# Another order of the attention units, and routing logits in fp32 by token

## The chip, the cores and the metric

The kernel runs on one core of a Trainium2 chip, alone. The metric is the time of one execution in device microseconds. Engines are named as the profile names them: PE is TensorE (PEld its weight loads), DVE is VectorE, ACT is ScalarE, POOL is GpSimd, SP is SyncE, whose queue issues most DMA transfers.

## The reference

Three stages in a row, all in fp32.

1. Gated linear attention, 4 batches, 8 heads, 768 positions, 48 wide: `state = f[t] * state + k[t] v[t]^T`, `y[t] = q[t] state`, with `f = sigmoid(f_logit)`.
2. A dense feed-forward layer on the 3072 tokens of 384 features (8 heads of 48): `h = x @ w_in` (384 to 2048), `g = h * clip(h + 3, 0, 6) / 6`, `x2 = g @ w_out`.
3. A mixture of 8 experts, one for each token:

```python
logits = x @ w_gate
e_idx = np.argmax(logits, axis=1)
gate_w = softmax(logits)[e_idx]
eom = 1.0 / (1.0 + np.exp(-(x @ w_output_gate)))
out[mask] = gate_w[mask, None] * eom[mask, e, None] * (np.maximum(x[mask] @ w1[e], 0.0) @ w2[e])
```

`x` in this third stage is the second stage's result. A logit that is off by a little can choose another expert, so the logits need full precision.

## The kernel before, in words

**Products in three parts.** Large matmuls run on fp32r operands, an fp32 number being split into a high and a low part (`split`, L122), and a product is three matmuls: high by high, high by low, low by high (`mm3`, L309 to L312).

**Attention units.** Tokens are cut into 8 blocks of 384 (half a batch). For each block there are four units, one for each pair of heads (`attention`, L212 to L306). A unit loads its f, k, q and v (L221, L223), makes decays on ScalarE and VectorE (L227 to L242), transposes k (L248), multiplies k by q (L253), masks (L260), multiplies k by v (L266), updates the state (L274 to L284) and sums the output `py` in PSUM (L291, L294), with head 0 of the pair in rows 0 to 47 and head 1 in rows 64 to 111. The output is split into high and low by ScalarE (L300) and VectorE (L301). The first products of a unit wait for that subtraction of the unit before (`freed`, L256).

**Where the output goes.** The feed-forward layer wants 384 features as 3 parts of 128 rows. Pairs 0, 1 and 2 are written straight into part 0, 1 and 2 of the block's tile `xx`, all 128 rows, of which 48 to 63 and 112 to 127 hold nothing. Pair 3 goes to a tile `yx`, and six DMA transfers on SP (L302 to L306) move 16 rows each from there into those free rows. Then every part is full. The pairs are taken in the order 0, 1, 2, 3.

**Feed-forward blocks.** `mlp` (L314) goes through 16 groups f of 128 hidden features: nine up matmuls over the three parts of `xx` into a PSUM bank `ph` (two banks in turn), `relu6` (ACT L347, DVE L348, ACT L349, DVE L350), and two groups later nine down matmuls into three accumulators (L323 to L325). Between groups the units of the coming blocks are written into the program: `UNITS = (-5, 0, 5, 9)` (L460) puts the second, third and fourth unit of block b + 1 at f = 0, 5 and 9, and the first unit of block b + 2 at f = 11. The units of block 0 and the first of block 1 come ahead of all blocks, in a prefix (L462 to L469), together with the first seven parts of the feed-forward weights; these are loaded as raw words into two buffers (L132) and converted by ScalarE and VectorE (L138 to L146). The other parts follow in the first groups of block 0.

**Routing.** After a block, `route` (L414) calls `choose` (L357). The accumulators are scaled into `row` (L363), transposed part by part (L366), and split into `xh` and `xl` (L367, L368). The logits come with the features on the output's rows: the stationary operand is the gate's weights, 32 columns (16 high beside 16 low), and the moving one is 384 tokens (L374, six matmuls). They are copied (L379), transposed back to tokens in three small steps (L382), copied and added (L385, L387). The weights for it are split beforehand (L470 to L476). Then come the choice of expert, a slot for each token, and three indirect DMA transfers that scatter the rows to DRAM (L436).

**Experts.** After the last block each expert's rows are loaded, transposed (L553) and put through two layers, the fullest expert first, its first 256 rows ahead of the others; those are transposed inside the last route (`meanwhile`). A general branch (L716 on), which these inputs don't enter, uses `choose` as well, with `keep`.

**What sets the order.** Instructions are given to a planner in program order; at compile time it fixes the order on each engine by that priority and by its own estimates of durations (`schedule_with_timeline_sim`, L868). `after_all` adds a wait, `in_turn` fixes an order on TensorE, `issue_after` places loads behind a given instruction. On the chip each engine follows its list. PSUM has three accumulator banks, two for `ph`, and three (`ps_m`) shared by attention, routing and transposes.

Of the kernel before, what the change touches and what calls it, by code (L numbers as in the profile page):

```python
# [10 lines left out]
F32 = mybir.dt.float32  # L11
F32R = mybir.dt.float32r
# [5 lines left out]
ALU = mybir.AluOpType  # L18
# [4 lines left out]
P = 128  # L23
# [3 lines left out]
KD = DM // P  # L27
FF = 2048
NF = FF // P
E = 8  # L30
FE = 1024
NFE = FE // P
TB = 384
# [15 lines left out]
def fused(ctx: ExitStack, tc: tile.TileContext, q, k, fl, v, vt, w_in, w_out, wg, w1, w2, out):  # L49
    nc = tc.nc  # L50
    const = ctx.enter_context(tc.tile_pool(name="const", bufs=1))
# [3 lines left out]
    ps_m = ctx.enter_context(tc.tile_pool(name="ps_m", bufs=3, space=PSUM))  # L55
# [17 lines left out]
    ident = const.tile([P, P], F32, name="ident")  # L73
# [33 lines left out]
    nc.gpsimd.memset(three, 3.0)  # L107
    gcmin = const.tile([R, 4 * NB], F32, name="gcmin")

    wgs = [const.tile([P, KD, 4 * E], F32R, name=f"wgs{i}") for i in range(2)]  # L110

    second = ExitStack()
    rtp = second.enter_context(tc.tile_pool(name="rtp", bufs=2))
# [5 lines left out]
    at1 = attc.enter_context(tc.tile_pool(name="at1", bufs=1, side="right"))  # L119
# [28 lines left out]
    def first_weights(pool):  # L148
        return [pool.tile(sh, F32R, name=n) for n, sh in (("wih", [P, KD, FF]), ("wil", [P, KD, FF]),
                                                          ("woh", [P, NF, DM]), ("wol", [P, NF, DM]))]  # L150
# [48 lines left out]
    sbds = []  # L199
    for i in range(2):  # L200
        t = at1.tile([R, NCH, 2, 64], F32, name=f"sbd{i}")
        nc.gpsimd.memset(t, 0.0)
        sbds.append(t)
    state, ready, freed = {}, [], []
# [7 lines left out]
    def attention(blk, pr, xx):  # L212
        b, half = divmod(blk, 2)
        n = 4 * blk + pr
        sbd = sbds[n % 2]
        qt = at2.tile([R, NCH, CH], F32, tag="qt", name="qt", bufs=3)
        kt = at2.tile([R, NCH, CH], F32, tag="kt", name="kt")
        xt = at2.tile([R, NCH, CH], F32, tag="xt", name="xt", bufs=3)
        vs = at2.tile([P, NCH, 2, 64], F32, tag="vs", name="vs")
        for t, src in ((xt, fl), (kt, k), (qt, q)):  # L220
            nc.sync.dma_start(out=t.rearrange("p c t -> p (c t)"),  # L221
                              in_=src[4 * b + pr, :, half * TB:(half + 1) * TB])
# [74 lines left out]
        in_turn(products)  # L297

        yx = xx[:, :, pr, :] if pr < 3 else at1.tile([P, 2, TB], F32R, tag="yx", name="yx")
        nc.scalar.copy(yx[:, 0, :], py)  # L300
        freed[1:] = [nc.vector.tensor_tensor(out=yx[:, 1, :], in0=py, in1=yx[:, 0, :].bitcast(F32), op=ALU.subtract)]  # L301
        if pr == 3:  # L302
            for j in range(KD):
                for x in range(2):
# [52 lines left out]
    def choose(pool, acc, keep=None, meanwhile=None):  # L357

        row = pool.tile([P, 3, ROW], F32, tag="row", name="row", bufs=1)
        xh, xl = (pool.tile([P, KD, TB], F32R, tag=n, name=n, bufs=1) for n in ("xTh", "xTl"))  # L360
        for t in range(3):
            ts_ = slice(t * P, (t + 1) * P)
            nc.scalar.activation(row[:, t, 0:DM], acc[t], AF.Copy, scale=1.0 / 6.0)  # L363
            px = ps_m.tile([P, KD, P], F32, tag="m", name="px")
            for kt in range(KD):
                nc.tensor.transpose(px[:, kt, :], row[:, t, kt * P:(kt + 1) * P], ident)  # L366
            nc.scalar.copy(xh[:, :, ts_], px)  # L367
            nc.vector.tensor_tensor(out=xl[:, :, ts_], in0=px, in1=xh[:, :, ts_].bitcast(F32), op=ALU.subtract)  # L368
        if keep is not None:
            keep(xh, xl)  # L370
        pl = ps_m.tile([4 * E, TB], F32, tag="m", name="pl")
        for i, (w, x) in enumerate(((wgs[0], xh), (wgs[1], xl))):
            for kt in range(KD):
                nc.tensor.matmul(pl, lhsT=w[:, kt, :], rhs=x[:, kt, :], start=i == 0 and kt == 0,  # L374
                                 stop=i == 1 and kt == KD - 1)
        if meanwhile is not None:
            meanwhile()
        lgT = pool.tile([4 * E, TB], F32, tag="lgT", name="lgT", bufs=1)
        nc.scalar.copy(lgT, pl)  # L379
        pt = ps_m.tile([P, 3, 4 * E], F32, tag="m", name="pt")  # L380
        for t in range(3):
            nc.tensor.transpose(pt[:, t, :], lgT[:, t * P:(t + 1) * P], ident[:4 * E, :4 * E])  # L382
        sm = lambda name, shape, dt=F32: pool.tile([P] + shape, dt, tag=name, name=name)
        lg2 = sm("lg2", [3, 4 * E])
        nc.vector.tensor_copy(lg2, pt)  # L385
        lg = sm("lg", [3, 2 * E])
        nc.vector.tensor_tensor(out=lg, in0=lg2[:, :, 0:2 * E], in1=lg2[:, :, 2 * E:], op=ALU.add)  # L387
        mx = sm("mx", [3, 1])
        nc.vector.tensor_reduce(out=mx, in_=lg[:, :, 0:E], op=ALU.max, axis=AX.X)
        dl = sm("dl", [3, E])  # L390
        nc.vector.tensor_tensor(out=dl, in0=lg[:, :, 0:E], in1=mx.to_broadcast([P, 3, E]), op=ALU.subtract)
        ex = sm("ex", [3, E])
        nc.scalar.activation(ex, dl, AF.Exp)
        se = sm("se", [3, 1])
        nc.vector.tensor_reduce(out=se, in_=ex, op=ALU.add, axis=AX.X)

        cand = sm("cand", [3, E])
        nc.vector.scalar_tensor_tensor(out=cand, in0=dl, scalar=0.0, in1=wts, op0=ALU.is_equal, op1=ALU.mult)
        m2 = sm("m2", [3, 1])
        nc.vector.tensor_reduce(out=m2, in_=cand, op=ALU.max, axis=AX.X)  # L400
        oh = sm("oh", [3, E], BF16)
        nc.vector.tensor_tensor(out=oh, in0=wts, in1=m2.to_broadcast([P, 3, E]), op=ALU.is_equal)

        zz = sm("zz", [3, E])
        nc.vector.tensor_tensor(out=zz, in0=lg[:, :, E:], in1=oh, op=ALU.mult)
        zs = sm("zs", [3, 1])
        nc.vector.tensor_reduce(out=zs, in_=zz, op=ALU.add, axis=AX.X)
        nc.scalar.activation(zs, zs, AF.Exp, scale=-1.0)
        nc.vector.tensor_scalar_add(zs, zs, 1.0)
        nc.vector.scalar_tensor_tensor(out=zs, in0=se, scalar=1e-9, in1=zs, op0=ALU.add, op1=ALU.mult)  # L410
        nc.vector.reciprocal(row[:, :, DM:DM + 1], zs)
        return row, oh
# [37 lines left out]

    xts = {}

    def att_unit(blk, pr):
        if pr == 0:
            xts[blk] = blkp.tile([P, 2, KD, TB], F32R, tag="xx", name="xx")
        attention(blk, pr, xts[blk])

    wfirst = first_weights(m1)

    UNITS = (-5, 0, 5, 9)  # L460
    parts = [part for i in range(NF // 4) for part in load_first(cv, i, *wfirst)]
# [5 lines left out]
    for pr in range(4):  # L467
        if UNITS[pr] < -1:
            att_unit(1, pr)  # L469
    wraw = at1.tile([P, KD, 4 * E], F32, name="wraw")  # L470
    nc.gpsimd.memset(wraw, 0.0)
    nc.sync.dma_start(out=wraw[:, :, 0:2 * E], in_=wg)
    nc.scalar.copy(wgs[1], wraw)
    nc.scalar.copy(wgs[0][:, :, 0:2 * E], wraw[:, :, 0:2 * E])
    nc.gpsimd.tensor_tensor(out=wgs[0][:, :, 2 * E:], in0=wraw[:, :, 0:2 * E],
                            in1=wgs[1].bitcast(F32)[:, :, 0:2 * E], op=ALU.subtract)  # L476

    def fill(e):
        fills.append(nc.sync.dma_start(out=xs_d[e * NT:e * NT + 384].rearrange("(j p) c -> p j c", p=P),
# [236 lines left out]
    with tc.If(general > 0):  # L716
# [41 lines left out]
        with ExitStack() as es:  # L758
            gp = es.enter_context(tc.tile_pool(name="gw", bufs=1))
            wg1 = first_weights(gp)  # L760
            for i in range(NF // 4):
                for part in load_first(gp, i, *wg1):
                    part()
            with tc.For_i(0, NB, 1) as nb:
                xg = gp.tile([P, KD, TB], F32, tag="xg", name="xg")
                xth = gp.tile([P, KD, TB], F32R, tag="xth", name="xgh")
                xtl = gp.tile([P, KD, TB], F32R, tag="xtl", name="xgl")
                yv = ya_d.rearrange("h (b r) p t -> (h b) r p t", r=4)
                for j in range(KD):
                    for x in range(2):  # L770
                        for dst, pr, src in ((64 * x, j, D * x), (64 * x + D, 3, D * x + 16 * j)):
                            n = D if pr < 3 else 16
                            nc.sync.dma_start(out=xg[dst:dst + n, j, :],
                                              in_=yv[bass.ds(nb, 1), pr, src:src + n].rearrange("a p t -> p (a t)"))
                split(xth, xtl, xg, nc.gpsimd)

                def keep(xh, xl):
                    x2 = gp.tile([P, KD, TB], F32, tag="x2", name="x2")
                    nc.vector.tensor_tensor(out=x2, in0=xh.bitcast(F32), in1=xl.bitcast(F32), op=ALU.add)
                    nc.sync.dma_start(out=x2_d[bass.ds(nb, 1)].rearrange("a p k t -> p (a k) t"), in_=x2)  # L780

                row, oh = choose(gp, mlp(gp, xth, xtl, *wg1, NF, relu6), keep)
                gs = gp.tile([P, E, 3, 2], F32, tag="gs", name="gs")
                nc.vector.tensor_copy(gs[:, :, :, 0], row[:, None, :, DM].to_broadcast([P, E, 3]))
                nc.vector.tensor_copy(gs[:, :, :, 1], oh.rearrange("p t e -> p e t"))
                for e in range(E):
                    nc.sync.dma_start(out=gs_d[e, bass.ds(nb, 1)].rearrange("a p t c -> p (a t) c"), in_=gs[:, e])
# [81 lines left out]
```

## Time and profile before

| | |
|---|---|
| median of 3 runs | 866.75 us (864.46 to 869.58) |
| the profiled execution | 864.98 us |
| its span in the profile | 863.3 us |
| mean granted clock of TensorE | 0.963 |
| TensorE busy | 805.9 us |
| VectorE busy | 526.4 us |
| ScalarE busy | 396.4 us |
| instructions | 14521 |

The span runs from the first to the last instruction; 1.7 us of the profiled execution lie around it. A timeline row gives the start in us from the span's start, the duration, the engine, the line, the operation, output and inputs by the program's names, the shape, how many instructions of the kind follow each other (then the duration is that of all), and in brackets the idle time of the engine before it with what ended it. `SPq` rows are DMA issues. Matmuls overlap their successors, so a matmul's own duration is longer than its share of the engine's time, which is read from start to start. [...]

### The profile page before, as it was taken

The numbers are of one execution on the slowest core, as the hardware profiler recorded it, in microseconds if no ns is written. First come the engines' busy times: TensorE is split into PE (matmuls) and PEld (weight loads), VectorE is DVE, ScalarE is ACT, GpSimd is POOL, SyncE is SP. The second block draws the span as 40 slices with busy tenths as digits, with TensorE's granted clock in tenths as the row PEclk, the third lists the DMA queues.
The fourth block names the chain that finished last, engine by engine and source line by source line (L and its number), as shares of the span: only waits on it lengthen the run. The fifth ranks groups of instructions, "written<-read, shape, count | busy, mean of one in ns | idle before, by whom it ended". The sixth has DMA issues, their size and how long they took to land.

```text
span 863.3 us, 14521 instructions
## 1 busy us (share of the span) xinstructions
PE 805.9 (93%) x5503; PEld 746.4 (86%) x5503; DVE 526.4 (61%) x1118; ACT 396.4 (46%) x843; POOL 62.3 (7%) x103
## 2 busy tenths in 40 slices
PE   7558998999998999999899999999999999999995
PEld 3338987998997998999799899899898999999994
DVE  6999975569554578654567843463464452554631
ACT  5556654447434455633445533453354342453520
POOL 2000000200010010010010010010100011101111
PEclk9558999999999999999999999999999999999998
DMA  6565495023021113110211200050254163255600
GB/s 200 169 187 156 153 283 168 29 68 106 1 70 52 31 62 92 48 61 26 65 63 42 57 29 11 14 174 20 68 178 157 34 207 131 92 185 183 216 26 28
DMA packets 42412, 85.01 MB, mean 98 GB/s; under 512 B 5954, under 2 KB 29795, under 8 KB 42333
## 3 DMA queue, kind: packets, MB, share of 16 engines
q1 hardware_dynamic: 39052, 74.50, 28.5%
q0 software_dynamic: 3280, 9.49, 3.0%
q8 instruction: 45, 0.74, 0.4%
q14 instruction: 35, 0.28, 0.1%
HBM read 65.77 MB, written 16.26 MB: 95 GB/s over the span
## 4 chain that ended last, share of the span: by engine, by line
PE 47%; DVE 4%; DMA 3%; ACT 2%; issue 1%; SPq 0%; POOL 0%; POOLq 0%; DVEq 0%; ACTq 0%
PE ph L310 7%; PE ph L312 7%; PE ph L311 7%; PE acc L323 3%; PE acc L324 3%; PE acc L325 3%; PE yacc L311 2%; PE yacc L312 2%; PE yacc L310 2%; DMA raw<-in_w 2%; PE yrow L599 1%; PE yrow L595 1%; PE yrow L598 1%; PE px L553 1%; PE py L291 1%
## 5 line engine op out<-in xcount | busy, mean ns | idle before, releaser
L310 PE MATMUL ph<-xx,wih 128*128 128x384 f32 x384 | 134.0, 349 | 9.8 <-DMA xx<-yx 6.5
L312 PE MATMUL ph<-xx,wil 128*128 128x384 f32 x384 | 132.6, 345 | 0.0
L311 PE MATMUL ph<-xx,wih 128*128 128x384 f32 x384 | 131.9, 344 | 0.0
L347 ACT ACTIVATE gf<-ph,three 128x384 f32<-128x384 f32 x128 | 73.6, 580 | 126.1 <-PE ph L312 122.9
L324 PE MATMUL acc<-wol,gh 128*128 128x384 f32 x384 | 129.8, 338 | 0.0
L323 PE MATMUL acc<-woh,gh 128*128 128x384 f32 x384 | 129.4, 337 | 0.3 <-ACT gh L349 0.3
L325 PE MATMUL acc<-woh,gl 128*128 128x384 f32 x384 | 122.0, 337 | 0.0
L348 DVE SCALAR_TENSOR_TENSOR gf<-gf,ph 128x384 f32<-128x384 f32 x128 | 70.1, 551 | 80.8 <-ACT gf L347 80.0
L350 DVE TENSOR_TENSOR gl<-gf,gh 128x384 fp32r<-128x384 f32 x128 | 70.4, 552 | 34.8 <-ACT gh L349 34.2
L354 DVE SCALAR_TENSOR_TENSOR hl<-ph,hh 128x256 fp32r<-128x256 f32 (+7 forms) x72 | 39.0, 542 | 82.2 <-ACT hh L353 77.2
L349 ACT CAST gh<-gf 128x384 fp32r<-128x384 f32 x128 | 65.3, 512 | 51.2 <-DVE gf L348 49.5
L310 PEld LDWEIGHTS ph<-xx,wih 128*128 128x128 f32 x384 | 74.2, 193 | 13.6 <-DMA xx<-yx 7.3
L353 ACT ACTIVATE hh<-ph 128x256 fp32r<-128x256 f32 (+7 forms) x72 | 34.6, 481 | 109.3 <-PE ph L312 109.3
L312 PEld LDWEIGHTS ph<-xx,wil 128*128 128x128 f32 x384 | 74.0, 193 | 0.9 <-issue 0.5
L311 PEld LDWEIGHTS ph<-xx,wih 128*128 128x128 f32 x384 | 74.0, 193 | 0.3
L323 PEld LDWEIGHTS acc<-woh,gh 128*128 128x128 f32 x384 | 72.1, 188 | 1.1 <-ACT gh L349 0.6
L324 PEld LDWEIGHTS acc<-wol,gh 128*128 128x128 f32 x384 | 72.1, 188 | 1.1 <-issue 0.7
L325 PEld LDWEIGHTS acc<-woh,gl 128*128 128x128 f32 x384 | 71.2, 188 | 0.8 <-issue 0.3
L310 PE MATMUL ph<-xh,w1h 128*128 128x256 f32 (+7 forms) x216 | 71.9, 334 | 0.0
L311 PE MATMUL ph<-xl,w1h 128*128 128x256 f32 (+7 forms) x216 | 71.7, 333 | 0.0
L312 PE MATMUL ph<-xh,w1l 128*128 128x256 f32 (+7 forms) x216 | 71.5, 332 | 0.0
L436 POOL DMA_INDIRECT xs_d<-row,sli x24 | 24.4, 1019 | 558.6 <-DVE sli L431 406.7
(168 smaller groups left out, 1471.0 us busy)
## 6 DMA issues: line engine op xcount, KB each, us to landing
raw<-in_w SPq DMA_DIRECT2D x23, 512.0 KB, 6.1
raw<-in_w SPq DMA_DIRECT2D x30, 384.0 KB, 3.4
vs<-in_v SPq DMA_DIRECT2D x32, 192.0 KB, 2.5
raw<-in_w_in SPq DMA_DIRECT2D x12, 512.0 KB, 4.2
raw<-in_w_out SPq DMA_DIRECT2D x12, 512.0 KB, 3.7
xt<-in_fl SPq DMA_DIRECT2D x32, 168.0 KB, 3.1
kt<-in_k SPq DMA_DIRECT2D x32, 168.0 KB, 2.3
qt<-in_q SPq DMA_DIRECT2D x32, 168.0 KB, 2.6
```

Of the source, the lines that this page charges most:

```text
L310: nc.tensor.matmul(ps, lhsT=wh, rhs=xh, start=first, stop=False)
L311: nc.tensor.matmul(ps, lhsT=wh, rhs=xl, start=False, stop=False)
L312: nc.tensor.matmul(ps, lhsT=wl, rhs=xh, start=False, stop=last)
L323: nc.tensor.matmul(acc[t], lhsT=gh[:, ts_], rhs=w2h[:, f, :], start=f == 0, stop=False)
L324: nc.tensor.matmul(acc[t], lhsT=gh[:, ts_], rhs=w2l[:, f, :], start=False, stop=False)
L325: nc.tensor.matmul(acc[t], lhsT=gl[:, ts_], rhs=w2h[:, f, :], start=False, stop=f == nf - 1)
L347: nc.scalar.activation(gf, ph, AF.Relu, bias=three)
L348: nc.vector.scalar_tensor_tensor(out=gf, in0=gf, scalar=6.0, in1=ph, op0=ALU.min, op1=ALU.mult)
L349: nc.scalar.copy(gh, gf)
L350: nc.vector.tensor_tensor(out=gl, in0=gf, in1=gh.bitcast(F32), op=ALU.subtract)
L353: return (nc.scalar.activation(gh, ph, AF.Relu).ins, nc.vector.scalar_tensor_tensor(out=gl, in0=ph, scalar=0.0, in1=gh.bitcast(F32), op0=A ...
L354: nc.vector.scalar_tensor_tensor(out=gl, in0=ph, scalar=0.0, in1=gh.bitcast(F32), op0=ALU.max, op1=ALU.subtract).ins)
```

## The change

The pairs are taken in the order 0, 1, 3, 2, so that the six transfers follow the third unit. Pair 2, now last, is written head by head into the rows that are its own, since the rows between may have been filled already; pair 0 and 1 are written as before. The two buffers `sbds` alternate by the number of units so far and not by the pair.

In `choose`, x2 is turned once and kept in fp32 (`xT`, one VectorE copy for each third), and the logits are fp32 matmuls with 128 tokens stationary and the 16 columns of the gate's weights moving, so that they come out by token. The split of the gate's weights, the second copy, the three small transposes and the addition go.

```diff
@@ fused @@
-    wgs = [const.tile([P, KD, 4 * E], F32R, name=f"wgs{i}") for i in range(2)]
+    wgs = const.tile([P, KD, 2 * E], F32, name="wgs")
@@ attention @@
-        sbd = sbds[n % 2]
+        sbd = sbds[len(ready) % 2]
...
-        nc.scalar.copy(yx[:, 0, :], py)
-        freed[1:] = [nc.vector.tensor_tensor(out=yx[:, 1, :], in0=py, in1=yx[:, 0, :].bitcast(F32), op=ALU.subtract)]
+        freed[1:] = []
+
+        for rows in heads if pr == 2 else (slice(0, P),):
+            nc.scalar.copy(yx[rows, 0, :], py[rows])
+            freed.append(nc.vector.tensor_tensor(out=yx[rows, 1, :], in0=py[rows], in1=yx[rows, 0, :].bitcast(F32),
+                                                 op=ALU.subtract))
@@ choose @@
-        xh, xl = (pool.tile([P, KD, TB], F32R, tag=n, name=n, bufs=1) for n in ("xTh", "xTl"))
+        xt = pool.tile([P, KD, TB], F32, tag="xT", name="xT", bufs=1)
...
-            nc.scalar.copy(xh[:, :, ts_], px)
-            nc.vector.tensor_tensor(out=xl[:, :, ts_], in0=px, in1=xh[:, :, ts_].bitcast(F32), op=ALU.subtract)
+            nc.vector.tensor_copy(xt[:, :, ts_], px)
+        pl = ps_m.tile([P, 3, 2 * E], F32, tag="m", name="pl")
+        for t in range(3):
+            for kt in range(KD):
+                nc.tensor.matmul(pl[:, t, :], lhsT=xt[:, kt, t * P:(t + 1) * P], rhs=wgs[:, kt, :], start=kt == 0,
+                                 stop=kt == KD - 1)
...
-        pl = ps_m.tile([4 * E, TB], F32, tag="m", name="pl")
-        for i, (w, x) in enumerate(((wgs[0], xh), (wgs[1], xl))):
-            for kt in range(KD):
-                nc.tensor.matmul(pl, lhsT=w[:, kt, :], rhs=x[:, kt, :], start=i == 0 and kt == 0,
-                                 stop=i == 1 and kt == KD - 1)
...
-        lgT = pool.tile([4 * E, TB], F32, tag="lgT", name="lgT", bufs=1)
-        nc.scalar.copy(lgT, pl)
-        pt = ps_m.tile([P, 3, 4 * E], F32, tag="m", name="pt")
-        for t in range(3):
-            nc.tensor.transpose(pt[:, t, :], lgT[:, t * P:(t + 1) * P], ident[:4 * E, :4 * E])
...
-        lg2 = sm("lg2", [3, 4 * E])
-        nc.vector.tensor_copy(lg2, pt)
         lg = sm("lg", [3, 2 * E])
-        nc.vector.tensor_tensor(out=lg, in0=lg2[:, :, 0:2 * E], in1=lg2[:, :, 2 * E:], op=ALU.add)
+        nc.vector.tensor_copy(lg, pl)
@@ att_unit, prefix @@
-    def att_unit(blk, pr):
-        if pr == 0:
+    def att_unit(blk, i):
+        pr = PAIRS[i]
+        if i == 0:
...
+    PAIRS = (0, 1, 3, 2)
...
-    wraw = at1.tile([P, KD, 4 * E], F32, name="wraw")
-    nc.gpsimd.memset(wraw, 0.0)
-    nc.sync.dma_start(out=wraw[:, :, 0:2 * E], in_=wg)
-    nc.scalar.copy(wgs[1], wraw)
-    nc.scalar.copy(wgs[0][:, :, 0:2 * E], wraw[:, :, 0:2 * E])
-    nc.gpsimd.tensor_tensor(out=wgs[0][:, :, 2 * E:], in0=wraw[:, :, 0:2 * E],
-                            in1=wgs[1].bitcast(F32)[:, :, 0:2 * E], op=ALU.subtract)
+    nc.sync.dma_start(out=wgs, in_=wg)
```

## Rows read from the trace of the kernel before

**Rows 1.** The page, its first part: busy time, share of the span and instructions by engine.

```profile
PE 805.9 (93%) x5503; PEld 746.4 (86%) x5503; DVE 526.4 (61%) x1118; ACT 396.4 (46%) x843; POOL 62.3 (7%) x103
```

**Rows 2.** Busy time by stage: stretch, its length, each engine's busy us, clock, DMA share, GB/s.

```profile
20.00:64.40 44.40, 23.61 (x157) 15.94 (x152) 41.81 (x86) 24.55 (x54) 0.00 (x0) 0.56 0.62 183
...
75.00:140.00 65.00, 61.79 (x464) 57.84 (x463) 57.64 (x118) 39.70 (x85) 0.00 (x0) 0.99 0.70 214
...
140.00:150.00 10.00, 9.26 (x44) 8.81 (x45) 3.89 (x9) 3.39 (x7) 0.00 (x0) 0.83 0.27 77
...
414.00:424.00 10.00, 9.21 (x58) 8.37 (x59) 8.21 (x16) 6.16 (x16) 0.00 (x0) 0.83 0.34 93
...
605.00:640.00 35.00, 33.33 (x274) 31.54 (x275) 17.45 (x52) 13.96 (x35) 4.92 (x5) 1.00 0.42 138
```

**Rows 3.** The waits of TensorE: who waited for whom, us in total, times, longest us.

```profile
PE ph L310 <- DMA xx<-yx: 6.5, 5, 2.6
...
PE ph L310 <- DVE gf L348: 2.9, 5, 1.0
...
PE pa L253 <- ACT kn L250: 1.8, 3, 0.8
```

**Rows 4.** The timeline where block 1 starts: start us, us, instruction, count, idle time before.

```profile
140.32 0.41 PE L310 MATMUL ph<-xx,wih 128*128 128x384 f32 x1 [2.58 <-DMA xx<-yx]
...
141.12 0.52 PE L311 MATMUL ph<-xx,wih 128*128 128x384 f32 x1
```

**Rows 5.** The timeline where block 5 starts.

```profile
411.55 0.94 PE L253 MATMUL pa<-qt,kb 48*128 48x128 f32 x12 [0.78 <-ACT kn L250]
...
414.38 0.66 PE L310 MATMUL ph<-xx,wih 128*128 128x384 f32 x1 [1.41 <-DMA xx<-yx]
```

**Rows 6.** The timeline of the prefix and of block 0's start.

```profile
47.14 7.20 SPq L132 DMA_DIRECT2D raw<-in_w_out  x3
...
60.79 0.54 DVE L301 TENSOR_TENSOR yx<-py,yx 128x384 fp32r<-128x384 f32 x1
...
61.36 3.94 SPq L305 DMA_DIRECT2D xx<-yx  x6
...
64.43 0.66 PE L310 MATMUL ph<-xx,wih 128*128 128x384 f32 x1 [0.75 <-DMA xx<-yx]
```

**Rows 7.** Instructions of the tile xx: ns min/median/max, first and last start.

```profile
L300 ACT CAST xx<-py x24: 457/480/483, 17.5 to 536.0; 128x384 fp32r<-128x384 f32 x24
...
L301 DVE TENSOR_TENSOR xx<-py,xx x24: 533/552/558, 18.0 to 536.5; 128x384 fp32r<-128x384 f32 x24
```

**Rows 8.** Groups by line and shape on TensorE: busy us, mean ns, idle before.

```profile
L253 PE MATMUL pa<-qt,kb 48*128 48x128 f32 x384 | 32.2, 303 | 4.0 <-ACT kn L250 1.8 <-ACT th L227 1.4 <-ACT th L230 0.8
```

**Rows 9.** The timeline of TensorE around the logits: block 0's route, then the last one.

```profile
135.62 0.42 PEld L291 LDWEIGHTS py<-at,vs 128*64 128x64 f32 x8 [0.25 <-issue]
...
147.70 0.69 PE L374 MATMUL pl<-xTh,wgs 128*32 128x384 f32 x3
...
148.22 0.34 PE L310 MATMUL ph<-xx,wih 128*128 128x384 f32 x1
...
608.85 0.19 PEld L311 LDWEIGHTS ph<-xl,w1h 128*128 128x128 f32 x1
...
608.96 0.19 PEld L312 LDWEIGHTS ph<-xh,w1l 128*128 128x128 f32 x1
...
609.21 0.19 PEld L312 LDWEIGHTS ph<-xh,w1l 128*128 128x128 f32 x1
...
609.53 0.37 PE L382 MATMUL pt<-ident,lgT 32*128 32x32 f32 x3
```

**Rows 10.** The timeline of the last route and of what follows it.

```profile
606.83 0.71 PE L374 MATMUL pl<-xTh,wgs 128*32 128x384 f32 x3 [0.59 <-ACT xTh L367]
...
608.33 0.47 ACT L379 COPY lgT<-pl 32x384 f32<-32x384 f32 x1 [0.16 <-PE pl L374]
...
628.67 0.39 PE L311 MATMUL yacc<-hl,w2h 128*128 128x256 f32 x1 [0.82 <-DVE hl L354]
```

More of the change, by code (lines that the diff above doesn't have):

```diff
@@ L366, in choose @@
                 nc.tensor.transpose(px[:, kt, :], row[:, t, kt * P:(kt + 1) * P], ident)
-            nc.scalar.copy(xh[:, :, ts_], px)
-            nc.vector.tensor_tensor(out=xl[:, :, ts_], in0=px, in1=xh[:, :, ts_].bitcast(F32), op=ALU.subtract)
-        if keep is not None:
-            keep(xh, xl)
-        pl = ps_m.tile([4 * E, TB], F32, tag="m", name="pl")
-        for i, (w, x) in enumerate(((wgs[0], xh), (wgs[1], xl))):
-            for kt in range(KD):
-                nc.tensor.matmul(pl, lhsT=w[:, kt, :], rhs=x[:, kt, :], start=i == 0 and kt == 0,
-                                 stop=i == 1 and kt == KD - 1)
+            nc.vector.tensor_copy(xt[:, :, ts_], px)
[4 more added lines that the diff above has]
+                                 stop=kt == KD - 1)
+        if keep is not None:
+            keep(xt)
         if meanwhile is not None:
             meanwhile()
-        lgT = pool.tile([4 * E, TB], F32, tag="lgT", name="lgT", bufs=1)
-        nc.scalar.copy(lgT, pl)
-        pt = ps_m.tile([P, 3, 4 * E], F32, tag="m", name="pt")
-        for t in range(3):
-            nc.tensor.transpose(pt[:, t, :], lgT[:, t * P:(t + 1) * P], ident[:4 * E, :4 * E])
         sm = lambda name, shape, dt=F32: pool.tile([P] + shape, dt, tag=name, name=name)
-        lg2 = sm("lg2", [3, 4 * E])
-        nc.vector.tensor_copy(lg2, pt)
         lg = sm("lg", [3, 2 * E])
-        nc.vector.tensor_tensor(out=lg, in0=lg2[:, :, 0:2 * E], in1=lg2[:, :, 2 * E:], op=ALU.add)
+        nc.vector.tensor_copy(lg, pl)
         mx = sm("mx", [3, 1])
@@ L775, in fused, with keep @@
                 split(xth, xtl, xg, nc.gpsimd)
-                def keep(xh, xl):
-                    x2 = gp.tile([P, KD, TB], F32, tag="x2", name="x2")
-                    nc.vector.tensor_tensor(out=x2, in0=xh.bitcast(F32), in1=xl.bitcast(F32), op=ALU.add)
+                def keep(x2):
                     nc.sync.dma_start(out=x2_d[bass.ds(nb, 1)].rearrange("a p k t -> p (a k) t"), in_=x2)
```

## The prediction, made before the changed kernel was run

> **What bounds the kernel now.** I read the page first, then busy time by stage, then the waits, then the timeline at the block starts. TensorE is busy for 93% of the span [rows 1], so the question is where the other 7% lies. [...] From 75 us on TensorE is busy nearly throughout (61.79 of 65.00 us). After that an edit is worth what it takes from or adds to TensorE's own work, or what idle time it closes.
>
> The waits name that idle time [rows 3]: five times the first up matmul of a block (L310) waits for the transfers that move the rows of heads 6 and 7 (yx to xx), 6.5 us in all, at most 2.6. It comes with a second loss. Before block 1 TensorE sits idle for 2.58 us; soon after, the same matmul's record grows to 0.52 us and the clock of that stretch is 0.83 instead of 1.00 [rows 2, 4]. Block 5 has the same 0.83 after idle times of 0.78 and 1.41 us [rows 2, 5]. At 0.83 over 10 us, 1.7 us of full-speed work is lost; twice makes 3.4 us.
>
> **The change part by part.**
>
> *The order of the units.* At the start of block 0 the last copy of the fourth unit starts at 60.79 and lasts 0.54, the six transfers go out from 61.36 to 65.30, and the first up matmul starts at 64.43 after a wait of 0.75 [rows 6]. With pair 3 third in line its six transfers leave about one unit earlier, so they have landed long before the block starts, and the first six up matmuls (parts 0 and 1 of xx) depend on nothing of the last unit. Gain: the 6.5 us, and the 3.4 us of clock if the idle time was what cost it. Late next is the last unit's own copy, which only the third part of xx needs. Ends: nothing gained if that copy takes the transfers' place, all of it otherwise. I take all, since six matmuls lie ahead of the part that needs it: 9.9 us.
>
> *Where the transfers go.* In every block the six issues (3.94 us of SP's queue, rows from 61.36 [rows 6]) pass ahead of whatever loads were behind the third unit. Later blocks have slack there: no weights are loaded in them. In the prefix they land among the raw weight loads, three of which issue from 47.14 over 7.20 us, paced by their two buffers [rows 6]. Behind them ScalarE and VectorE would wait for raw weights. I take zero, as the queue itself is waiting for buffers there; ends 0 and 3.9 us.
>
> *Head by head.* Pair 2's copy becomes two on ScalarE and two on VectorE with the same columns on 48 rows. A copy of all 128 rows takes 0.48 us, the subtraction 0.55 [rows 7]; the added pair has the same 384 columns on fewer rows, so I charge the full price, 0.48 and 0.55 per block. What hides it is the time before the block starts; what doesn't is the next unit's first products (L253), which wait for this very subtraction: before block 5 that wait is already open (0.78) [rows 5], and three such waits come to 1.8 us [rows 3], of which I put two at a block's end. Two times 0.55 = +1.1 us; ends 0 (the planner puts up matmuls there) and three times 1.03.
>
> *Logits, TensorE.* Removed per block: six matmuls with 384 moving columns, three of which take 0.52 us from their first start to the next matmul's start (147.70 to 148.22), so 1.04; and three small transposes, some 0.3 [rows 9]. Together 1.35 us. Added: nine fp32 matmuls with 128 stationary and only 16 moving columns. An fp32 matmul here is two instructions: the program's 192 products at L253 (32 units, three chunks, two heads) stand in the trace as 384 [rows 8], with a weight load each. So 18 loads of 128 columns with almost nothing to hide behind. Loads of that size start 0.11 us apart at the closest (608.85, 608.96) and 0.125 apart on the next two (to 609.21) [rows 9]. 18 times 0.11 is 2.0 us, so +0.63 per block; at 0.125, +0.9. The other end: eight loads of half the columns take 0.42, or 0.053 each [rows 9], which would make it 0.95 us and a gain of 0.4. I take 0.11, the row of the same size. In seven blocks TensorE has no idle time to absorb it: +4.4 us (ends -2.8 and +6.3).
>
> *Logits, the other engines.* Three casts to xh (0.48 each, as in [rows 7]) and the copy of lgT (0.47 [rows 10]) leave ScalarE; on VectorE three subtractions become three copies of the same shape (same price), and two small steps become one. ScalarE thus does 1.9 us less just where a block starts, and where up matmuls wait for the activation to give back a bank: 2.9 us in five waits [rows 3]. I take a quarter of it, -0.7; ends 0 and -2.9.
>
> *The last route.* Here TensorE waits: 0.59 us ahead of the logits, which hides their 0.63 extra, and 0.82 us at 628.67 after the rows that this route scatters came late [rows 10]. The chain from acc to slots loses a cast of 0.48, the copy of 0.47 and the transposes, over 1 us. I take -0.8; ends 0 and -1.4.
>
> *Preparing the gate weights.* One DMA straight into place; two narrow casts leave ScalarE, each at most the 0.48 of a copy four times as wide [rows 7]. I take zero, because VectorE bounds the prefix [rows 2] and hides it; ends 0 and -1.0.
>
> **Sum.** -6.5 - 3.4 + 1.1 + 4.4 - 0.7 - 0.8 = -5.9 us. On the profiled execution's 864.98 that is 859.1. The median of the runs is 866.75, 1.8 above it; the forecast goes with the median: 860.9.
>
> **The rivals.**
>
> *More than that.* The planner now has six ready up matmuls at each boundary and puts them into the waits at L253 (1.8 [rows 3]), the 1.1 isn't paid, and block 0 starts some 2 us sooner because TensorE idles in the prefix. Another -4.9: 856.0. For: those matmuls hang on nothing late. Against: older units come first in the program.
>
> *The last copy takes the transfers' place.* VectorE is in order and busy; before block 0 its copy was late. Half of the 9.9 stays: 865.9.
>
> *Raw loads late in the prefix.* The 3.9 us of issues hold up weights on the engine that bounds that stage: 864.8.
>
> *The clock falls in the route.* Nine transposes and 18 short matmuls give TensorE 3 us in which few columns stream, once per block. The price is 1.7 us per fall, as in blocks 1 and 5 [rows 2]; eight falls cost 13.6: 874.5, slower. It decides from six falls on (10.2 us, the forecast's gain plus 4.3). Against: nine transposes and two idle times in the last route left the clock at 1.00 (605 to 640) [rows 2]. [...]
>
> *Loads that hide behind nothing.* If each of the 18 pays its load's full 0.19 us [rows 9], a block pays 3.4 and not 2.0: +16.3 in place of +4.4 over eight blocks, 872.8. Against: loads of 0.19 that start 0.11 apart [rows 9]. [...]
>
> *The transfers stay last.* The planner may still let unit and transfers end at the block's start: no 9.9, 870.8.
>
> **How the numbers follow.** Forecast 0.38; more 0.20; last copy 0.13; raw loads 0.13; clock 0.08; transfers stay last 0.05; loads 0.03. The range 854 to 869 leaves out the last three and a tail of the second. A measurement of this kernel can tell about 0.5%, 4.3 us, from no change: faster is under 862.4, slower over 871.1. Faster: two thirds of the forecast's case (0.26), all of the second, and small parts of the next two (0.07): 0.53. Slower: most of the clock's case, the loads' and half of the transfers' (0.12), and a little for a plan that came out badly in some other way: 0.14. The rest, 0.33, is the same.
>
> **What would show it.** In the changed profile: no row "PE ph L310 <- DMA xx<-yx"; a clock of 1.00 in the ten us after blocks 1 and 5 start; the six transfers of a block well before its first up matmul; 18 logit instructions per block with loads some 0.11 us apart, about 2 us in all; ScalarE's busy time down by about 12 us. It is wrong if first up matmuls wait for L301 as long as they did for the transfers, if VectorE waits longer for raw weights between 45 and 60 us, or if the granted clock dips after the routes.

## The result, and the profile after

The changed kernel takes 857.81 us (855.66 to 858.24, 4 runs) beside 865.61 for the kernel before (864.46 to 869.58): a ratio of 0.9908, 95% interval 0.9882 to 0.9934. The forecast was 860.9; it started from 866.75, the median of three runs before, of which this comparison has four. The profiled execution took 857.86, its span is 856.1; before it was 864.98, so 7.1 us went. By stage of the two traces:

| stage | before, us | after, us |
|---|---|---|
| start to the first up matmul | 64.4 | 50.6 |
| block 0's up matmuls | 65.0 | 79.6 |
| block 0's last up to the last route | 474.9 | 470.3 |
| of that: TensorE idle / lost to the lower clock / the rest | 14.1 / 3.4 / 457.4 | 6.6 / 3.4 / 460.3 |
| last route to the end | 258.9 | 255.6 |

(Idle is the sum of the gaps ahead of TensorE's instructions; lost is time at half clock, halved.) Block 0 starts 14 us sooner and its up matmuls end 0.8 us later: by these rows the earlier start is worth nothing (a run below tries it). The 7.1 us lie in the blocks (4.6) and behind the last route (3.3), less that 0.8.

The changed kernel's page, busy time by engine, answers to [rows 1]:

```profile
PE 807.9 (94%) x5575; PEld 753.9 (88%) x5575; DVE 528.3 (62%) x1118; ACT 388.0 (45%) x817; POOL 59.3 (7%) x101
```

TensorE has 72 instructions more, nine a block, and is busy 2.0 us longer; ScalarE lost 8.4 us, where about 12 were forecast. The waits of TensorE over the whole span, answering to [rows 3] (in all, times, longest):

```profile
PE py L291 <- ACT sbd L284: 12.4, 6, 4.8
PE ph L314 <- DVE gf L352: 8.9, 4, 5.6
...
PE ph L314 <- DMA xx<-yx: 2.3, 1, 2.3
PE pa L253 <- DVE xx L304: 1.7, 1, 1.7
...
```

The transfers are waited for once, ahead of block 0, instead of five times. Waits for the state that a unit needs (sbd) were there before too; from block 0's last up matmul to the last route the kernel before has

```profile
PE ph L310 <- DMA xx<-yx: 5.8, 4, 2.6
PE py L291 <- ACT sbd L284: 2.7, 3, 1.2
```

and the changed kernel has 5.6 us for sbd, in three waits, each some 8 us behind the start of block 2, 4 or 6, where the next block's first unit needs that state. So 5.8 us of waits went there and 2.9 came. And the clock falls again. Busy time by stretch, answering to [rows 2]; the columns are those of [rows 2]:

```profile
20.00:50.60 30.60, 18.46 (x128) 12.11 (x125) 28.00 (x57) 16.19 (x34) 0.00 (x0) 0.60 0.61 181
...
132.00:142.00 10.00, 10.00 (x89) 8.85 (x87) 3.34 (x8) 3.57 (x8) 0.00 (x0) 1.00 1.04 352
...
211.80:215.20 3.40, 3.40 (x29) 3.07 (x26) 2.21 (x5) 2.13 (x5) 0.00 (x0) 0.50 0.31 82
```

Block 1's start (132.1) now has full clock and no idle time, against 0.83 in [rows 2]. But from 211.8 it is 0.50 for 3.4 us, right behind a 1.85 us wait for sbd (the row at 211.54 below), and again at 484.9 behind one of 1.95. Two falls before, two after: 3.4 us lost in both.

The logits and the last route, answering to [rows 9, 10] (start us, us, instruction, count):

```profile
601.06 1.31 PE L370 MATMUL px<-ident,row 128*128 128x128 f32 x9 [0.28 <-ACT row L367]
601.64 1.49 DVE L371 COPY xT<-px 128x384 f32<-128x384 f32 x3 [3.14 <-PE px L370]
602.25 1.41 PEld L375 LDWEIGHTS pl<-wgs,xT 128*128 128x128 f32 x12
602.25 1.51 PE L375 MATMUL pl<-wgs,xT 128*128 128x16 f32 x12
...
603.87 0.74 PE L375 MATMUL pl<-wgs,xT 128*128 128x16 f32 x6
604.46 0.42 PE L546 MATMUL px<-ident,xr 128*128 128x128 f32 x2
604.81 0.20 DVE L383 COPY lg<-pl 128x48 f32<-128x48 f32 x1
```

Nine products are 18 instructions with 18 loads. From first start to the next matmul's start a run of six takes 0.59 us here (603.87 to 604.46), and one of twelve 1.26 in the route behind block 1 (220.03 to 221.29, below), so 1.85 us a block against some 1.35 before. The route is shorter: from row's first copy (600.5) to lg's end it is 4.5 us, where it took 6.1.

The two timelines below are of the start of block 3, in the changed kernel, and then of the route that follows block 1:

```profile
269.41 0.47 ACT L303 CAST xx<-py 48x384 fp32r<-48x384 f32 x1 [1.96 <-PE py L294]
...
269.84 0.44 ACT L250 COPY kn<-pk 128x336 f32<-128x336 f32 x1
269.91 0.55 DVE L304 TENSOR_TENSOR xx<-py,xx 48x384 fp32r<-48x384 f32 x1 [1.88 <-ACT xx L303]
...
271.39 0.47 ACT L303 CAST xx<-py 48x384 fp32r<-48x384 f32 x1
...
271.98 0.56 DVE L304 TENSOR_TENSOR xx<-py,xx 48x384 fp32r<-48x384 f32 x1
...
275.82 0.94 PE L253 MATMUL pa<-qt,kb 48*128 48x128 f32 x12
```

```profile
211.54 0.49 PE L291 MATMUL py<-at,vs 128*64 128x128 f32 x4 [1.85 <-ACT sbd L284]
...
214.10 1.40 PE L370 MATMUL px<-ident,row 128*128 128x128 f32 x6
...
219.18 0.49 PE L370 MATMUL px<-ident,row 128*128 128x128 f32 x3
...
220.03 1.41 PE L375 MATMUL pl<-wgs,xT 128*128 128x16 f32 x12
...
221.29 0.42 PE L315 MATMUL ph<-xx,wih 128*128 128x384 f32 x1
```

The last unit's second copy (271.39) comes 2 us after its first: kn and an activation (270.78) stand between them on ScalarE. The next unit's first products (L253) need both subtractions. They start at 275.82, which is 3.3 us after the second has ended (272.54), and TensorE is busy until then: what puts them there is the order on TensorE, which was fixed at compile time, and not a wait on the chip. In the second timeline a first unit that is late in this way meets the route: its products (py, 211.54) stand right in front of the route's transposes (214.10), with which they share the three ps_m banks, and the last three transposes come 5 us after the first six.

### The profile page after: what moved, and what is told of

Its sections match the earlier page's. It is cut to its first block, busy times and chain, and to the rows that moved or that the text cites. A ratio compares the mean times of both kernels' runs of the same rounds, so it can differ in the third digit from the quotient of the medians.

```text
span 856.1 us, 14631 instructions
## 1 busy us (share of the span) xinstructions
PE 807.9 (94%) x5575; PEld 753.9 (88%) x5575; DVE 528.3 (62%) x1118; ACT 388.0 (45%) x817; POOL 59.3 (7%) x101
## 4 chain that ended last, share of the span: by engine, by line
PE 80%; DVE 11%; DMA 4%; issue 2%; ACT 2%; SPq 1%; POOL 0%; POOLq 0%; DVEq 0%; ACTq 0%
PE ph L314 11%; PE ph L316 11%; PE ph L315 11%; PE acc L327 7%; PE acc L328 7%; PE acc L329 7%; PE py L291 3%; PE yacc L315 3%; PE yacc L316 3%; PE yacc L314 3%; PE pa L253 2%; PE py L294 2%; PE pl L375 2%; DMA raw<-in_w_in 1%; PE yrow L592 1%
## 5 line engine op out<-in xcount | busy, mean ns | idle before, releaser
L327 PE MATMUL acc<-woh,gh 128*128 128x384 f32 x384 | 131.2, 342 | 0.0
L329 PE MATMUL acc<-woh,gl 128*128 128x384 f32 x384 | 124.3, 337 | 0.2 <-DVE gl L354 0.2
L354 DVE TENSOR_TENSOR gl<-gf,gh 128x384 fp32r<-128x384 f32 x128 | 70.6, 552 | 31.7 <-ACT gh L353 30.9
```

The source lines that it names most:

```text
L327: nc.tensor.matmul(acc[t], lhsT=gh[:, ts_], rhs=w2h[:, f, :], start=f == 0, stop=False)
L329: nc.tensor.matmul(acc[t], lhsT=gl[:, ts_], rhs=w2h[:, f, :], start=False, stop=f == nf - 1)
L354: nc.vector.tensor_tensor(out=gl, in0=gf, in1=gh.bitcast(F32), op=ALU.subtract)
```

## The experiments

All ratios are to the kernel before in runs on the same chip. "Stage" is block 0's last up to the last route, "route" the mean time from row's first copy to lg's end over the six routes of blocks 0 to 5. Every kernel got its own order at compile time, so an edit can move more than what it names.

| kernel | order of pairs | last unit | logits | median us | ratio (95%) | stage us | idle / lost clock | route |
|---|---|---|---|---|---|---|---|---|
| before | 0123 | whole | split, by feature | 865.61 | 1 | 474.9 | 14.1 / 3.4 | 20.5 |
| after | 0132 | by head | fp32, by token | 857.81 | 0.9908 (0.9882–0.9934) | 470.3 | 6.6 / 3.4 | 15.3 |
| order only | 0132 | by head | as before | 886.23 | 1.0246 (1.0224–1.0268) | 496.3 | 24.5 / 17.1 | 30.9 |
| logits only | 0123 | whole | as after | 848.69 | 0.9816 (0.9796–0.9836) | 459.1 | 1.1 / 0.0 | 12.0 |
| fp32 by feature | 0123 | whole | fp32, by feature | 865.71 | 1.0019 (1.0001–1.0037) | 476.2 | 9.0 / 3.4 | 18.6 |
| split by token | 0123 | whole | split, by token | 852.93 | 0.9886 (0.9862–0.9909) | 464.7 | 4.8 / 1.7 | 14.8 |
| ScalarE load | 0123 | whole | as after | 847.66 | 0.9811 (0.9789–0.9834) | 461.8 | 2.1 / 1.7 | 12.5 |
| heads only | 0123 | by head | as after | 855.36 | 0.9916 (0.9891–0.9940) | 463.4 | 4.1 / 0.0 | 12.3 |
| whole copies | 0132 | whole | as after | 845.97 | 0.9794 (0.9771–0.9817) | 456.8 | 0.0 / 0.0 | 11.5 |

**The two halves alone.** The kernel before with the order and the copies by head of the change, its logits untouched:

```
-        nc.scalar.copy(yx[:, 0, :], py)
+        for rows in heads if pr == 2 else (slice(0, P),):
+            nc.scalar.copy(yx[rows, 0, :], py[rows])
...
+    PAIRS = (0, 1, 3, 2)
```

> Only the order 0, 1, 3, 2 with the last unit written head by head; logits as before. My theory: the order brings all of the gain and more, since the logits cost TensorE time (1.85 us per block in the changed trace against 1.35 before, seven blocks exposed: 3.5 us). So about 3 us below the changed kernel, some 855 us at the changed kernel's 857.8. Rival: the logits bring a part of the gain through a shorter route and less work on ScalarE and VectorE; then the order alone gives less than the whole change, 859 to 862 us.

Measured: 886.23 us, slower by 2.5%, against either expectation. Its waits of TensorE:

```profile
PE py L291 <- ACT sbd L284: 16.3, 5, 4.8
PE ph L314 <- DVE gf L352: 12.7, 7, 5.6
PE ph L314 <- ACT xx L303: 10.7, 5, 3.0
PE pa L253 <- DVE xx L304: 4.8, 4, 1.8
...
PE ph L314 <- DMA xx<-yx: 0.9, 1, 0.9
```

The transfers are gone from the block starts and the last unit's copy stands there (10.7 us in five waits, each ahead of the thirteenth up matmul of its block, the first that needs that copy); at the three longest of these waits the clock falls to 0.50, and stays there for 10 to 14 us. What the order and what the copies by head do of this was not separated under the old logits. Then the logits of the change alone, pairs in the old order and copied whole:

```
-        for rows in heads if pr == 2 else (slice(0, P),):
-            nc.scalar.copy(yx[rows, 0, :], py[rows])
...
+        nc.scalar.copy(yx[:, 0, :], py)
...
-    PAIRS = (0, 1, 3, 2)
+    PAIRS = (0, 1, 2, 3)
```

> Only the fp32 logits by token with the plain load of the gate's weights; order 0, 1, 2, 3 as before. My theory: +3.5 us on TensorE less about 1.5 for the last route and the shorter waits at block starts, so 1 to 3 us above the kernel before (867 to 869 at its 865.6). Rival: the logits alone are faster than before by 1 to 4 us (862 to 865).

Measured: 848.69 us, below either expectation. The part that I had priced as a loss gains 1.8%, twice what the whole change gains. Its waits from 64 us on, and the transfers and first up matmul of block 3:

```profile
PE py L291 <- ACT sbd L284: 2.9, 1, 2.9
PE ph L310 <- DMA xx<-yx: 1.9, 2, 1.0
PE ph L310 <- DVE gf L348: 0.9, 1, 0.9
...
```

```profile
264.62 3.78 SPq L305 DMA_DIRECT2D xx<-yx  x6
...
272.44 0.33 PE L310 MATMUL ph<-xx,wih 128*128 128x384 f32 x1
```

The fourth unit's transfers are still last, but they go out 8 us ahead of the block. The waits that the new order was to remove go by themselves once the route is shorter.

**What in the logits gains?** The shorter chain, or the casts that left ScalarE? Three kernels. One keeps fp32 but goes back to logits by feature, with the copy to lgT and the second transposes:

```
+        for kt in range(KD):
+            nc.tensor.matmul(pl, lhsT=wgs[:, kt, :], rhs=xt[:, kt, :], start=kt == 0, stop=kt == KD - 1)
...
+        nc.scalar.copy(lgT, pl)
...
+            nc.tensor.transpose(pt[:, t, :], lgT[:, t * P:(t + 1) * P], ident[:2 * E, :2 * E])
```

> The logits-only kernel with its logits laid out by feature again: fp32 without a split, gate weights stationary, 384 tokens moving (3 products), then the ScalarE copy to lgT and 3 small transposes as in the kernel before. Rows go in the order 0,1,2,3. Theory A (what gained in the logits-only kernel is the shorter chain between the last x2 piece and lg: no lgT copy, no second transposes, one PSUM tile less): it falls back to most of the kernel before, 860 us or more. Theory B (what gained is that the split's three casts left ScalarE): within 3 us of the logits-only kernel, 846 to 852 us.

One keeps the split with all its casts, but makes the logits by token, so lgT and pt go:

```
+                    nc.tensor.matmul(pl[:, t, :], lhsT=x[:, kt, t * P:(t + 1) * P], rhs=w[:, kt, :],
+                                     start=i == 0 and kt == 0, stop=i == 1 and kt == KD - 1)
```

> The kernel before with its split kept (three ScalarE casts, three VectorE subtractions a block, rows in the order 0,1,2,3), but the logits made by token: 18 products with slices of x stationary and 32 gate columns moving, so that the lgT copy and the 3 small transposes go. Theory A (the shorter chain gains): 853 us or less, most of the way to the logits-only kernel. Theory B (the casts that left ScalarE gain): within 5 us of the kernel before, 860 us or more.

And one gives the logits-only kernel its ScalarE work back, as three copies that nothing reads:

```
             nc.vector.tensor_copy(xt[:, :, ts_], px)
+            nc.scalar.copy(pool.tile([P, KD, P], F32, tag="spare", name="spare", bufs=1), xt[:, :, ts_])
```

> The logits-only kernel with three spare ScalarE copies of x2's transposed pieces a block (384 columns each, some 0.48 us, so 1.4 us a block as the casts had), whose result nothing reads. Theory A (the shorter chain gains, ScalarE's load does not matter): 847 to 852 us, within 3 us of the logits-only kernel. Theory B (the casts that left ScalarE gain): 856 us or more, half of the gain or more given back.

Measured: 865.71, 852.93 and 847.66 us. All three go with theory A. ScalarE's load is worth nothing that can be told (0.9811 against 0.9816); by token alone gives 1.1%; fp32 by feature gives nothing. In fp32 by feature some of the loss is TensorE's own: with 384 moving columns it runs six instructions of 0.34 us each, 2.04 us from start to start where by token it is 1.85,

```profile
223.21 2.11 PE L370 MATMUL pl<-xT,wgs 128*16 128x384 f32 x6
...
225.35 0.47 ACT L376 COPY lgT<-pl 16x384 f32<-16x384 f32 x1 [0.68 <-PE pl L370]
```

but of its 17.1 us on the logits-only kernel in the stage, 7.9 are idle time and 3.4 clock. lgT and pt take 0.47 and 0.37 us [rows 9, 10], but with them gone the mean route falls by 5.7 us, from 20.5 to 14.8. Whether the ps_m bank that pt took or the extra hop over ScalarE matters more was not separated.

**What does the order cost, then?** The change has all that the logits-only kernel has, and is 0.9% slower. First theory: with nothing late holding them, the next block's up matmuls go ahead of this block's last down matmuls. One order on TensorE forbids it:

```
+                if between is not None and f == 0 and kt == 0 and ends:
+                    tc.add_manual_dep(one.ins, ends[-1].ins.name, ORDER, reason="one block after the other")
```

> The changed kernel with one order and no wait added: on TensorE the first up matmul of a block stands behind the last down matmul of the block before. Theory A (the new row order harms because the next block's up matmuls, which no transfer holds any more, go ahead of this block's last down matmuls, so that route and attention start later): 850 us or less, near the logits-only kernel. Theory B (the harm is the last unit's own extra work, its two pairs of copies on ScalarE and VectorE and the square of spatial rows that comes free later): within 4 us of the changed kernel, 854 to 862 us.

Measured: 857.23 us, ratio 0.9928 (0.9909 to 0.9948): no gain. The waits for sbd fall from 5.6 to 0.3 us, but the down matmuls then wait for the activations (3.6 and 1.4 us). That theory fell. Two more that moved nothing: the units issued earlier, and block 0's start held back to where the transfers held it before.

```
-    UNITS = (-5, 0, 5, 9)
+    UNITS = (-5, 0, 4, 8)
```

> The changed kernel with its third and fourth unit of a block issued one feature block earlier (UNITS -5,0,4,8 for -5,0,5,9). Theory A (the units come too late against the route of their block, so that the first unit of the next block meets the route in the three banks): 852 us or less. Theory B (the number issued does not set when they come): 855 to 860 us, within 3 us of the changed kernel.

```
+                if between is not None and f < 3 and kt == 0 and len(marks) < 8:
+                    tc.add_manual_dep(one.ins, marks[4][-1].ins.name, ORDER, reason="first block behind the fifth unit")
```

> The changed kernel with one order and no wait added: on TensorE the first up matmuls of block 0 stand behind the last pkv product of the fifth unit, so that block 0 starts some 12 us later, as it did when transfers held it. Theory A (the units fall behind once, in block 0, whose up matmuls go first when no transfer holds them, and stay behind for the run): 852 us or less, most of the way to the logits-only kernel. Theory B (the units fall behind in each block anew): 855 us or more, the start of block 0 itself being worth under 2 us either way.

Measured: 856.19 us, ratio 0.9929 (0.9898 to 0.9959), and 856.73, 0.9925 (0.9904 to 0.9947): theory B both times. Held, block 0 starts at 66.0 instead of 50.6 and its last up matmul ends at 130.7 instead of 130.2.

What was left is the copies by head. They were taken out of the change, and put into the logits-only kernel, each alone:

```
-        for rows in heads if pr == 2 else (slice(0, P),):
+        for rows in (slice(0, P),):
```

> The changed kernel with the last unit's rows copied and subtracted whole (one copy, one subtraction) and not head by head; the row order 0,1,3,2 and the fp32 logits stay. Theory A (what the change loses against the logits-only kernel lies in when the units come, not in the copies' number): 854 to 861 us, within 3 us of the changed kernel. Theory B (the two pairs of copies, through the squares and banks that they hold longer, cost it): 851 us or less.

(The whole copy writes over the 16 rows in each half of part 2 that the transfers had filled, so those rows of x are not the reference's; the instructions behind it are the same, and the stretch behind the last route takes 256.7 us against 255.6.)

```
+        for rows in heads if pr == 3 else (slice(0, P),):
+            nc.scalar.copy(yx[rows, 0, :], py[rows])
```

> The logits-only kernel (row order 0,1,2,3) with the copy and the subtraction of the last unit's rows made head by head, as the change does for its last unit. Theory A (the copies' number does not matter): 846 to 851 us, within 3 us of the logits-only kernel. Theory B (it is what the change loses): 854 us or more.

Measured: 845.97 and 855.36 us, theory B in both. Copies by head cost 1.1% in the new order (0.9794 to 0.9908) and 1.0% in the old (0.9816 to 0.9916), 9 to 10 us; that two orders with their own plans agree speaks against an accident of one plan. With the logits of the change, the order as such is worth 0.1 to 0.2%, within the intervals. In the old order's two traces, 4.3 of the 6.7 us lie in the stage, and 2.9 ahead of block 0's last up matmul, where TensorE sits idle for 6.3 us ahead of L253 (67.47) until the subtraction is done. The same block start as above, with whole copies:

```profile
260.31 0.48 ACT L303 CAST xx<-py 128x384 fp32r<-128x384 f32 x1 [0.40 <-PE py L294]
...
260.74 0.44 ACT L250 COPY kn<-pk 128x336 f32<-128x336 f32 x1
260.83 0.56 DVE L304 TENSOR_TENSOR xx<-py,xx 128x384 fp32r<-128x384 f32 x1 [0.32 <-ACT xx L303]
...
264.99 0.94 PE L253 MATMUL pa<-qt,kb 48*128 48x128 f32 x12
```

From the first copy to the next unit's L253 it is 4.7 us, against 6.4 with two pairs. Over blocks 2 to 7 the first unit goes from its transposes (pk) to L253 in 4.5 us here and 6.8 in the changed kernel: 2.3 us a block, and the stage differs by 13.5 over six such starts. In the old order the same step is 6.2 us with copies by head and 4.9 without. With whole copies TensorE has no idle time between block 0's last up and the last route, and the clock stays at 1.00 there. This kernel's waits from 128 us to the end:

```profile
PE yrow L592 <- DVE hl L358: 0.9, 1, 0.9
PE yacc L315 <- DVE hl L358: 0.7, 2, 0.6
PE px L370 <- ACT row L367: 0.3, 1, 0.3
PE px L546 <- DMA xr<-xs_d: 0.2, 1, 0.2
```

That the late L253 carries the whole cost is read from these rows and not shown: a kernel whose next unit needs less was not tried. Nor is it shown why the order puts L253 so late; here too it starts 3.6 us after the subtraction has ended (261.39), with TensorE busy between, so it keeps about the same distance from the last subtraction in both kernels.

**TensorE's price of the logits, doubled.**

```
-            for kt in range(KD):
+            for kt in [*range(KD)] * 2:
```

> The changed kernel with each of the nine logit matmuls of a block done twice, the second overwriting the first: 18 more instructions, 1.85 us of TensorE per block. If every us of TensorE after block 0 counts, the time rises by seven or eight times 1.85, 13 to 15 us (871 to 873). Rival: the logits lie beside waits of TensorE; then the rise is under half of that, below 7 us (865).

(Each slice's three products are made twice, the second time over the first.) Measured: 882.71 us, ratio 1.0216 (1.0187 to 1.0245): 24.9 us more than the changed kernel, against 14 expected. The stage's work rises by 13.3, as it should; its lost clock rises from 3.4 to 13.7, while its idle time falls from 6.6 to 1.1; 5.2 us more lie behind the last route's start, where by the falls counted below another 3.4 are lost to the clock. Here is where the clock goes (two routes; columns as in [rows 2]):

```profile
221.20:225.60 4.40, 4.40 (x41) 4.40 (x40) 2.12 (x4) 2.48 (x6) 0.00 (x0) 1.00 0.01 4
226.20:229.60 3.40, 3.40 (x13) 3.40 (x12) 2.37 (x12) 1.10 (x4) 0.00 (x0) 0.50 0.00 0
290.30:294.50 4.20, 4.20 (x40) 4.20 (x38) 1.02 (x2) 0.01 (x1) 0.00 (x0) 0.99 0.00 0
294.50:297.90 3.40, 3.40 (x12) 3.40 (x13) 1.51 (x9) 0.75 (x3) 0.00 (x0) 0.50 0.00 0
```

TensorE is never idle in these rows, yet right behind 36 short matmuls its clock is at 0.50 for 3.4 us. It falls behind or within seven of the eight routes' logits, four times for 3.4 us and three times for 6.8; with 18 in the changed kernel it fell behind none (the clock is 1.00 from 215.2 to 484.8 and from 488.3 to 850).

**Is VectorE the prefix's bound?** The changed kernel with the weights' subtraction moved to GpSimd:

```
-        nc.vector.tensor_tensor(out=lo, in0=t.bitcast(F32), in1=hi.bitcast(F32), op=ALU.subtract)
+        nc.gpsimd.tensor_tensor(out=lo, in0=t.bitcast(F32), in1=hi.bitcast(F32), op=ALU.subtract)
```

> The changed kernel with the subtraction that makes the low part of the first layer's weights (24 times 0.68 us, L146) on GpSimd in place of VectorE. Theory that VectorE bounds the prefix and block 0 (115 of 130 us busy in both kernels, last up matmul of block 0 at 129.4 before and 130.2 after although its first started 14 us earlier): 16 us less on VectorE, time falls by 5 to 12 us (846 to 853). Rival: TensorE's own work or its clock bounds block 0; then the time stays within 2 us of the changed kernel.

Measured: 858.69 us, ratio 0.9925 (0.9906 to 0.9944): no gain, the time that the rival named. Groups of this kernel (busy us, mean ns):

```profile
L260 DVE TENSOR_TENSOR at<-pa,nmask 128x384 f32<-128x384 f32 x64 | 32.9, 551 | 22.2 <-PE pa L253 22.1
...
L140 DVE SCALAR_TENSOR_TENSOR s<-raw,s 128x512 uint32<-128x512 uint32 x24 | 22.0, 917 | 0.1
L237 DVE TENSOR_TENSOR rg<-r,gg 112x384 f32<-112x384 f32 x32 | 20.0, 625 | 0.6
...
L146 POOL TENSOR_TENSOR wil<-s,wih 128x512 fp32r<-128x512 f32 x12 | 18.7, 1560 | 46.3 <-ACT wih L145 46.3
```

and of the changed kernel:

```profile
L260 DVE TENSOR_TENSOR at<-pa,nmask 128x384 f32<-128x384 f32 x64 | 32.9, 551 | 24.8 <-PE pa L253 24.7
L237 DVE TENSOR_TENSOR rg<-r,gg 112x384 f32<-112x384 f32 x32 | 17.8, 555 | 0.5
...
L140 DVE SCALAR_TENSOR_TENSOR s<-raw,s 128x512 uint32<-128x512 uint32 x24 | 16.3, 678 | 0.0
L146 DVE TENSOR_TENSOR wol<-s,woh 128x512 fp32r<-128x512 f32 x12 | 8.2, 684 | 0.7 <-ACT woh L145 0.7
```

The 16.4 us that left VectorE come back as slower instructions beside GpSimd's: VectorE is busy 532.1 us in this kernel and 528.3 in the changed one. Each subtraction takes 1.53 to 1.56 us on GpSimd instead of 0.68, and block 0's last up matmul ends at 137.7 instead of 130.2. So VectorE was not relieved, and this run does not tell whether it bounds the prefix. The stage behind is 5.0 us shorter than in the changed kernel, which makes up for most of block 0's delay; why is open.

## Why the prediction was right and wrong

The time lies 3.1 us below the forecast and inside its range; the reasons mostly do not hold. Two errors of opposite sign met: the order with its copies was priced at -8.8 us and costs some 8 (+0.9%), the logits were priced at +2.9 and gain some 16 (-1.8%). That the total is near is luck. The rival "more than that" (856.0) comes nearer still, but of its three reasons only one held: the waits at L253 are gone from the blocks, while the copies by head are paid and the early start of block 0 gives nothing.

- **The transfers (-6.5).** The wait is gone from the block starts, as predicted, but the order did not win the time. Alone, with the old logits, the order (with its copies) costs 2.5%, and the rival "the last copy takes the transfers' place" is what its waits show. The step that failed is "I take all, since six matmuls lie ahead": TensorE had done twelve, and the copy still came up to 3.0 us later; the last unit itself was late, not only its transfers. With the shorter route and whole copies either order is on time: 1.1 us idle in the stage with the old, none with the new.
- **The clock (-3.4).** Not gained: the two falls moved behind the waits for sbd.
- **Head by head (+1.1).** Mis-sized: 9 to 10 us. I charged two instructions at their own duration and two waits. I did name who waits for that subtraction (L253), and rightly: [rows 5] puts the 0.78 down to kn, but kn is done at 411.30 and the subtraction at 411.45. I did not follow that unit on through the block, where, as the timeline behind block 1 suggests, it meets the route in the three ps_m banks.
- **Logits on TensorE (+4.4).** Right: 0.50 us a block against 0.63, so +3.5 over seven blocks. The loads are 105 and 98 ns apart, by the row that I took (0.11). The rival of loads that hide behind nothing is out.
- **Logits elsewhere (-0.7).** The failed step on the other side: I counted the instructions removed, engine by engine, and not the chain that they were. The lgT and pt steps cost 1.1% of the run; with fp32 as well, and so without the split and lg2, it is 1.8%. That the time comes back through the attention units behind the route is read from the columns "idle" and "route", and not shown by a run of its own. ScalarE's relief, of which I took a quarter, is worth nothing by the spare copies.
- **The last route (-0.8).** 3.3 us in the traces, and 3.4 in the logits-only kernel: right in sign, the chain again.
- **The prefix (0).** Right. Started 14 us sooner or held, block 0 ends at the same time; and between 40 and 66 us VectorE waits for raw words once, 1.4 us before and 1.5 after, so raw loads came no later there.
- **The clock falls in the route (a rival, 8%).** Not at 18 short matmuls; at 36 it does, and the price of 1.7 us a fall (half of 3.4) was right for four of the seven falls, the other three costing 3.4. Nine transposes with 18 matmuls left the clock at 1.00 in the last route (601 to 640); no run has transposes alone.

By parts, in per cent of the run: the logits -1.8, the copies by head +1.0 to 1.1, the order itself about -0.1. These are steps along one path from the kernel before to the changed one, so that they add up to the measured -0.9 is no further test; under the old logits the order and the copies cost 2.5% together and not 0.9.

## What to carry to other kernels

Price a step that is removed by the chain that it stood in, and follow that chain until something else is late: two small steps of 0.8 us together made the route 5.7 us longer. Where an instruction is split in two, look at what waits for the second half and what the engine's order puts between the halves. Undo each part of a change by itself: this one hid a 1.8% gain behind a 1% loss, and the logits alone (0.9816) beat the whole.

## What the runs showed of the hardware

With the logits doubled, a busy TensorE lost its clock: behind or within 36 fp32 matmuls of 16 columns, nine transposes ahead of them, it was at 0.50 in seven routes of eight, for 3.4 or 6.8 us. In the two of these routes shown above TensorE was busy throughout (4.40 us of 4.40 with 41 instructions, 4.20 of 4.20 with 40).

With the weights' subtraction on GpSimd some of VectorE's groups were slower in the mean: L140 and L237, with two inputs in SBUF, went from 678 to 917 ns and from 555 to 625, while L260, with one input in PSUM, stayed at 551 (its 14 instructions in the stretch with the subtractions took 549 in both kernels). Of L140's 24 instructions the twelve that overlap such a subtraction take 1159 ns in the mean, at most 1735, and the other twelve 675. That the place of the inputs makes the difference was not tried by itself.
